# Second MLP: the order of matrix products and output tiles on TensorE, per pair of chunks

## The chip, the cores and the metric

The program runs on one core of one Trainium2 chip. The metric is the device time of one execution in microseconds (us), the median of the runs shown. The core has five engines that run side by side: TensorE (PE in the profile; its weight loads are listed apart as PEld), VectorE (DVE), ScalarE (ACT), GpSimd (POOL) and SyncE (SP), which issues the DMAs here. Each engine works through its own list of instructions in order, and semaphores hold an instruction back until what it needs is there.

## What is computed

Attention with a linear kernel, whose result is the input of a first MLP, whose result is the input of a second one. The change lies in the second MLP alone.

```python
def _moe2_ref(x, w_in, w_out):          # x 4608 x 512, w_in 512 x 2048, w_out 2048 x 512
    h = x @ w_in
    g = h * (1.0 / (1.0 + np.exp(-1.702 * h)))
    return (g @ w_out).astype(np.float32)
```

## The kernel before, in words

**Precision.** A float32 product is made of three matmuls of split operands: each operand is kept as a high part (`to_hi`, a copy on ACT) and a low part (`to_lo`, a subtraction on DVE or POOL), and `three` (L616) issues high by high, high by low, low by high. So every row `x3` or `x6` of TensorE is one or two products of 128x128 weights.

**Tokens and chunks.** The second MLP goes over 4608 tokens in six blocks of 768 (`NB2`), each of two halves of 384 tokens (`TH`). The 2048 columns of `w_in` are 16 chunks of 128, taken in eight pairs (`NQ`). A step of the work is one pair of chunks of one block; the text calls it pair n, n from 0 to 47, and pairs 8, 16, 24, 32 and 40 are the first of blocks 1 to 5.

**The first layer of a pair.** `x @ w_in` for 2 by 2 blocks (two halves of tokens, two chunks) is made with seven products instead of eight, on sums and differences of the operands. `steps_l1` (L764) lists them with their times in units of `PT` (2.2 us): the products a11, s2, a12, s3, s1, a22, s4, of six matmuls of 384 columns each. They accumulate in two PSUM buffers of the pool `ps_h` (two buffers, tag "h"), in three tiles per pair: bank 0 takes a11, then a12; bank 1 takes s2, s3 and a22; a second bank-0 tile takes s1 and s4. In the profile the first is called pa, the others ps. Between two products on one tile DVE or ACT reads the intermediate sum:

- `m1` (L798, ACT) copies a11's result; `add` (L805, DVE) makes c12 from bank 1 after s2, c22 from bank 1 after s3 and once more from bank 0 after s1, c21 from bank 1 after a22, c12 again from bank 0 after s4.
- `act` (L816, L817) is the activation of each of c11, c22, c21, c12: a sigmoid on ACT, a multiplication on DVE. `split` makes the high and low part of g, called gc in the profile (ACT and POOL, L134 and L137).

A product that goes on in a tile must wait until the read before it is done, and a product that begins a tile waits for the last reader of the buffer's tile before.

**The second layer.** While pair n's products run, the g blocks of pair n - 1 are multiplied by `w_out`: `unit` (L857) is one token tile (128 tokens) of one g block: three matmuls of 512 columns, added to one of six accumulators in PSUM (tiles 0 to 2 for the first half of the tokens, 3 to 5 for the second). A pair has twelve units, in the order c11 (tiles 0 to 2), c22 (3 to 5), c12 (0 to 2), c21 (3 to 5). The table `UNITS` (L1008) gives each of the twelve a time in `PT`, and so the place among the products.

**The end of a block.** In pairs 8, 16, 24, 32 and 40 the units finish the block before: tiles 0 to 2 with c12, tiles 3 to 5 with c21. `put_2` (L878), called right behind each unit's place, copies a finished tile to SBUF, even tiles on ACT (L892), odd ones on DVE (L894), and issues the DMA to the output.

**What sets the order.** Every step is put in a list with a time (`at`, L143); L1021 sorts the list by time and calls the steps in that order. So the times move instructions in all five lists of instructions, but no engine looks at them when it runs.

**Around the first pairs.** Other work shares the engines in pairs 0 to 8: the last sums and splits of the first layer's weights (`steps_q`, L295), the splitting of `w_out` (`steps_o`, L273: load, high on ACT, low on POOL, store), and in pairs 7, 15, 23 and so on the sums and splits of the next block's tokens (`steps_s`, L704).

Of the kernel before, what the change touches and what calls it, by code (L numbers as in the profile page):

```python
# [58 lines left out]
def kernel(  # L59
# [73 lines left out]
    def to_hi(hi, src):  # L133
        nc.scalar.activation(hi, src, AF.Copy)  # L134

    def to_lo(lo, src, hi, eng=nc.vector):
        eng.tensor_tensor(out=lo, in0=src, in1=hi.bitcast(F32), op=ALU.subtract)  # L137
# [5 lines left out]
    def at(t, fn, *args):  # L143
        plan.append((t, len(plan), fn, args))
# [471 lines left out]
    def three(out, w, x, start, stop, shared=False):  # L616

        for e, (a, b) in enumerate(((0, 0), (0, 1), (1, 0))):
            nc.tensor.matmul(  # L619
                out, w(a), x(b), start=(start and e == 0), stop=(stop and e == 2), skip_group_check=shared  # L620
            )
# [142 lines left out]
    def steps_l1(n):  # L764


        st = {}
        i, j = divmod(n, NQ)

        def product(bank, x, begin):  # L770
            def run():
                if begin:
                    st[bank] = ps_h.tile([P, TB], F32, tag="h", name=f"p{x}_{n}")
                a, at0 = W_AT[x]
                w, xs = wt[a, j], x_t["2", i, x]
                for k in range(2):
                    cs = slice(at0 + k * P, at0 + (k + 1) * P)
                    three(
                        st[bank][:, :TH],
                        lambda e: w[:, e, cs],  # L780
                        lambda e: xs[:, e, k, :],
                        begin and k == 0,
                        k == 1,
                        shared=True,
                    )

            return run

        def tile_(name):
            pool, tag = dict(  # L790
                m1=(late, "m1"), c12=(late, "c12"), c22=(late, "c22"), c21=(None, "t"), c11=(None, "t"), s=(None, "g")
            )[name]
            pool = cpool if pool is None else late["pool"]
            return pool.tile([P, TH], F32, tag=tag, name=f"{name}_{n}", bufs=2 if tag in ("c12", "t", "g") else 1)

        def m1():
            st["m1"] = tile_("m1")
            nc.scalar.activation(st["m1"], st[0][:, :TH], AF.Copy)  # L798

        def add(name, bank, to):  # L800
            def run():
                other = st[to]
                if name not in st:
                    st[name] = tile_(name)
                nc.vector.tensor_tensor(out=st[name], in0=st[bank][:, :TH], in1=other, op=ALU.add)  # L805

            return run

        def act(name):
            def run():  # L810
                if name == "c11":
                    h = st[0][:, :TH]
                    sig = st[name] = tile_(name)
                else:
                    h, sig = st[name], tile_("s")
                nc.scalar.activation(sig, h, AF.Sigmoid, scale=1.702)  # L816
                nc.vector.tensor_tensor(out=st[name], in0=h, in1=sig, op=ALU.mult)  # L817

            return run

        def split(name):
            def run():

                last = (name == "c12") == (n % 2 == 0) and name in ("c12", "c21")
                pool, tag = (late["pool"], "g4") if last else (gpool, "g")
                g = pool.tile([P, 2, TH], F32R, tag=tag, name=f"g{name}_{n}")
                to_hi(g[:, 0, :], st[name])
                to_lo(g[:, 1, :], st[name], g[:, 0, :], nc.gpsimd)
                g_t["2", n, name] = g

            return run

        return [
            (0.0, product(0, "a11", True)),
            (0.48, m1),
            (1.0, product(1, "s2", True)),
            (1.5, add("c12", 1, "m1")),
            (2.0, product(0, "a12", False)),
            (2.5, act("c11")),
            (3.0, product(1, "s3", False)),  # L840
            (3.1, split("c11")),
            (3.5, add("c22", 1, "m1")),
            (4.0, product(0, "s1", True)),
            (4.5, add("c22", 0, "c22")),
            (4.55, act("c22")),
            (5.0, product(1, "a22", False)),
            (5.1, split("c22")),
            (5.5, add("c21", 1, "m1")),
            (5.55, act("c21")),
            (6.0, product(0, "s4", False)),  # L850
            (6.1, split("c21")),
            (6.5, add("c12", 0, "c12")),
            (6.55, act("c12")),
            (7.1, split("c12")),
        ]
# [43 lines left out]
    with tc.manual_schedule():  # L899
# [11 lines left out]
        def when(t0, times, steps):  # L911
            for t, fn in zip(times, steps.values(), strict=True):
                at(t0 + t, fn)
# [82 lines left out]
        for i in range(NB2):  # L996
# [5 lines left out]
            else:  # L1002
# [2 lines left out]
                times += [0.6 * PT if i < 2 else quad(NQ * i - 2) + 3.7 * PT - t]  # L1005
                times += [e * PT for e in (0.5, 1.55, 2.55, 1.6, 3.6, 4.6, 5.6, 6.6)]
                when(t, times, steps_s(i))
        UNITS = [0, 0, 1, 1, 2, 2, 3, 3, 4, 4, 5, 6]  # L1008
        for n in range(NB2 * NQ + 1):
            if n < NB2 * NQ:  # L1010
                for dt, fn in steps_l1(n):
                    at(quad(n) + dt * PT, fn)
                for e in range(2 if n >= NQ else 0):
                    at(quad(n) + (0.3 + 0.1 * e) * PT, load_o, n // NQ, 2 * (n % NQ) + e)
            if n:
                order = ("c11", "c22", "c12", "c21") if n < NB2 * NQ else ("c11", "c22", "c21", "c12")
                todo = [(c, t) for c in order for t in range(NT2 // 2)]
                for e, (c, t) in zip(UNITS, todo, strict=True):
                    at(quad(n) + (e + 0.47) * PT, unit, n - 1, c, t)
                    at(quad(n) + (e + 0.49) * PT, put_2)  # L1020
# [32 lines left out]
```

## Time and profile before

| | |
|---|---|
| median of 3 runs | 1681.07 us (1680.23 to 1681.24) |
| the profiled execution, from its first to its last instruction (span) | 1678.0 us |
| TensorE busy in it | 1637.8 us, 98% |
| DVE, ACT, POOL busy | 935.7, 670.4, 697.7 us (56%, 40%, 42%) |
| second MLP: first product, last matmul's end | 907.2, 1674.1 us |

A row of the timeline reads: start in us from the span's start, duration in us, engine, line, operation, out<-in by the program's names with numbers left out, shape, how many equal instructions follow each other, and in square brackets the idle time of the engine before and what ended it. Matmuls overlap: the duration of a group runs to the end of its last one, so the pace is read from start to start. A row of the windows view reads: the stretch, its length, then TensorE's busy time and number of instructions (or all engines'), the granted TensorE clock as a share of full speed (PEclk), the DMA share and GB/s.

### The profile page before, as it was taken

How to read it: one execution, taken by the hardware profiler on the slowest of the kernel's cores; microseconds unless marked ns; L12 is line 12 of the kernel's file. 1: busy time of each engine (PE TensorE's matmuls, PEld its weight loads, DVE VectorE, ACT ScalarE, POOL GpSimd, SP SyncE). 2: the span in 40 equal slices, each digit the busy share in tenths (PEclk: the TensorE clock that was granted, in tenths of full speed). 3: DMA queues.
4: the chain of work that ended last, by engine and by line, in shares of the span. 5: the costliest groups of instructions: out<-in, count | busy, mean ns of one | idle time of the engine just before them, and what ended most of it. 6: DMA issues, size and time to landing. Idle time of an engine off the chain costs nothing.

```text
span 1678.0 us, 21576 instructions
## 1 busy us (share of the span) xinstructions
PE 1637.8 (98%) x7848; PEld 1407.0 (84%) x7848; DVE 935.7 (56%) x1647; ACT 670.4 (40%) x1228; POOL 697.7 (42%) x589
## 2 busy tenths in 40 slices
PE   6889999999999999999999999999999999999999
PEld 5667888888888888888887898888888888898897
DVE  8985767767676766666456434334334334334333
ACT  5655443444444444443434334324324324324322
POOL 4656333343334333333478546225225235235222
PEclk9989999999999999999999999999999999999999
DMA  7652323233322223211222323412412412412212
GB/s 214 186 155 75 96 65 106 74 100 90 105 81 80 85 83 96 66 57 50 75 78 82 143 88 113 151 51 77 150 51 80 146 51 82 144 52 84 104 53 86
DMA packets 127914, 159.75 MB, mean 95 GB/s; under 512 B 54080, under 2 KB 90944, under 8 KB 127808
## 3 DMA queue, kind: packets, MB, share of 16 engines
q1 hardware_dynamic: 127808, 158.37, 29.1%
q8 instruction: 62, 1.02, 0.2%
q14 instruction: 44, 0.36, 0.1%
HBM read 122.68 MB, written 35.65 MB: 94 GB/s over the span
## 4 chain that ended last, share of the span: by engine, by line
PE 84%; DVE 2%; POOL 2%; issue 2%; ACT 1%; DMA 1%; SPq 0%; POOLq 0%; ACTq 0%; DVEq 0%
PE acc L619 42%; PE ph L619 20%; PE ps L619 14%; PE pa L619 5%; PE px L574 1%; PE pk L440 1%; DVE qt L537 1%; POOL gc L137 1%; DMA to<-wod 0%; DVE c L817 0%; POOL wo L137 0%; ACT s L134 0%; DVE o L675 0%; DVE a L137 0%; ACT s L816 0%
## 5 line engine op out<-in xcount | busy, mean ns | idle before, releaser
L619 PE MATMUL acc<-wo,gc 128*128 128x512 f32 x1728 | 453.4, 394 | 0.0
L619 PE MATMUL acc<-g,wo 128*128 128x512 f32 x1728 | 423.2, 394 | 2.2 <-DVE to L209 0.9
L619 PE MATMUL ph<-x,wi 128*128 128x512 f32 x1728 | 422.5, 393 | 0.1
L619 PEld LDWEIGHTS acc<-g,wo 128*128 128x128 f32 x1728 | 324.2, 189 | 71.1 <-POOL g L137 1.5
L619 PEld LDWEIGHTS ph<-x,wi 128*128 128x128 f32 x1728 | 322.0, 189 | 67.3 <-PE warm L940 0.2
L137 POOL TENSOR_TENSOR gc<-c,gc 128x384 fp32r<-128x384 f32 x192 | 201.1, 1049 | 422.6 <-ACT gc L134 416.1
L619 PEld LDWEIGHTS acc<-wo,gc 128*128 128x128 f32 x1728 | 319.3, 188 | 46.1
L137 POOL TENSOR_TENSOR g<-g,g 128x512 fp32r<-128x512 f32 x144 | 195.9, 1360 | 382.2 <-ACT g L134 342.7
L134 ACT ACTIVATE g<-g 128x512 fp32r<-128x512 f32 x144 | 90.9, 631 | 207.0 <-DVE g L644 206.9
L805 DVE TENSOR_TENSOR c<-ps,m 128x384 f32<-128x384 f32 x144 | 80.2, 557 | 165.6 <-PE ps L619 152.8
L644 DVE TENSOR_TENSOR g<-g 128x512 f32<-128x512 f32 x128 | 108.3, 846 | 112.7 <-ACT g L638 110.3
L817 DVE TENSOR_TENSOR c<-c,s 128x384 f32<-128x384 f32 x144 | 100.4, 697 | 101.2 <-ACT s L816 101.2
L134 ACT ACTIVATE gc<-c 128x384 fp32r<-128x384 f32 x192 | 101.0, 526 | 135.9 <-DVE c L817 133.2
L816 ACT ACTIVATE s<-c 128x384 f32<-128x384 f32 x144 | 75.5, 524 | 193.9 <-DVE c L805 191.6
L638 ACT ACTIVATE g<-ph 128x512 f32<-128x512 f32 x144 | 85.6, 595 | 156.9 <-PE ph L619 154.2
L537 DVE STREAM_TRANSPOSE qt<-q 32x128 f32<-32x128 f32 x448 | 135.5, 302 | 5.7
L619 PE MATMUL pa<-a,w 128*128 128x384 f32 x576 | 117.2, 338 | 3.1 <-DVE c L805 1.8
L619 PE MATMUL ps<-s,wa 128*128 128x384 f32 x576 | 115.9, 335 | 2.4 <-DVE c L805 2.4
L619 PEld LDWEIGHTS pa<-a,w 128*128 128x128 f32 x576 | 103.0, 188 | 13.9 <-ACT m L798 3.0
L619 PEld LDWEIGHTS ps<-s,wa 128*128 128x128 f32 x576 | 102.9, 188 | 11.6 <-DVE c L805 3.2
L805 DVE TENSOR_TENSOR c<-ps,c 128x384 f32<-128x384 f32 x96 | 53.3, 555 | 67.1 <-PE ps L619 67.1
L817 DVE TENSOR_TENSOR c<-pa,c 128x384 f32<-128x384 f32 x48 | 26.7, 556 | 91.0 <-ACT c L816 90.4
(114 smaller groups left out, 1695.6 us busy)
## 6 DMA issues: line engine op xcount, KB each, us to landing
wo<-wod SPq DMA_DIRECT2D x80, 512.0 KB, 4.0
rawi<-in_moe_w_in_dram SPq DMA_DIRECT2D x32, 512.0 KB, 4.4
rawo<-in_moe_w_out_dram SPq DMA_DIRECT2D x32, 512.0 KB, 3.9
y<-o SPq DMA_DIRECT2D x36, 256.0 KB, 2.8
out_dram<-o SPq DMA_DIRECT2D x36, 256.0 KB, 2.0
k<-in_k_dram SPq DMA_DIRECT2D x32, 256.0 KB, 4.0
vt<-in_v_dram SPq DMA_DIRECT2D x64, 128.0 KB, 3.1
wod<-wo SPq DMA_DIRECT2D x16, 512.0 KB, 2.8
```

The lines of the kernel that those rows point to most:

```text
L134: nc.scalar.activation(hi, src, AF.Copy)
L137: eng.tensor_tensor(out=lo, in0=src, in1=hi.bitcast(F32), op=ALU.subtract)
L440: nc.tensor.matmul(st["pk"][:, :VW], st["ke"][:, j, :], st["v"][:, j, :], start=(j == 0), stop=(j == KJ),)
L537: nc.vector.transpose(out=st["qt"][32 * g : 32 * g + 32, a * P : (a + 1) * P].rearrange("d (j t) -> d j t", j=QJ), in_=st["qn"][32 * a : 3 ...
L574: nc.tensor.matmul(st["px"][:, cols], a, c[:, cols], start=(e == 0), stop=(e == 2))
L619: nc.tensor.matmul(out, w(a), x(b), start=(start and e == 0), stop=(stop and e == 2), skip_group_check=shared)
L638: nc.scalar.activation(st["g"], st["h"], AF.Relu)
L644: nc.vector.tensor_tensor(out=st["g"], in0=st["g"], in1=st["g"], op=ALU.mult)
L805: nc.vector.tensor_tensor(out=st[name], in0=st[bank][:, :TH], in1=other, op=ALU.add)
L816: nc.scalar.activation(sig, h, AF.Sigmoid, scale=1.702)
L817: nc.vector.tensor_tensor(out=st[name], in0=h, in1=sig, op=ALU.mult)
```

## The change

The times of three products in `steps_l1` move so that each stands right behind the product before it, and `UNITS` puts the three token tiles of one g block together. The order becomes: a11, s2, three units of c11; a12, s3, three of c22; s1, a22, three of c12; s4, three of c21. Nothing is added or removed.

```diff
@@ steps_l1
             (0.0, product(0, "a11", True)),
             (0.48, m1),
-            (1.0, product(1, "s2", True)),
+            (0.4, product(1, "s2", True)),
             (1.5, add("c12", 1, "m1")),
             (2.0, product(0, "a12", False)),
             (2.5, act("c11")),
-            (3.0, product(1, "s3", False)),
+            (2.4, product(1, "s3", False)),
             (3.1, split("c11")),
             (3.5, add("c22", 1, "m1")),
             (4.0, product(0, "s1", True)),
             (4.5, add("c22", 0, "c22")),
             (4.55, act("c22")),
-            (5.0, product(1, "a22", False)),
+            (4.4, product(1, "a22", False)),
...
-        UNITS = [0, 0, 1, 1, 2, 2, 3, 3, 4, 4, 5, 6]
+        UNITS = [0, 0, 0, 2, 2, 2, 4, 4, 4, 6, 6, 6]
```

On TensorE, the first ten groups of pair 16. The names: pa11, ps2 and ps1 are the three tiles of the first layer; after the arrow stands the product's operand (a11, s2, ...); acc2 with block and token tile is an accumulator, gc11 and so on the g block with its pair. Before:

```order
L619 MATMUL pa11_16_10068<-a11_2_9949,w10_7394 128x384 x6
L619 MATMUL acc2_1_0_9213<-wo2_1_14_9937,gc11_15_9995 128x512 x3
L619 MATMUL acc2_1_1_9217<-wo2_1_14_9937,gc11_15_9995 128x512 x3
L619 MATMUL ps2_16_10090<-s2_2_9967,wq0_7488 128x384 x6
L619 MATMUL acc2_1_2_9230<-wo2_1_14_9937,gc11_15_9995 128x512 x3
L619 MATMUL acc2_1_3_9234<-wo2_1_15_9939,gc22_15_10035 128x512 x3
L619 MATMUL pa11_16_10068<-a12_2_9986,w10_7394 128x384 x6
L619 MATMUL acc2_1_4_9246<-wo2_1_15_9939,gc22_15_10035 128x512 x3
L619 MATMUL acc2_1_5_9250<-wo2_1_15_9939,gc22_15_10035 128x512 x3
L619 MATMUL ps2_16_10090<-s3_2_10006,wa0_7449 128x384 x6
```

TensorE, the same place now:

```order
L619 MATMUL pa11_16_10068<-a11_2_9959,w10_7394 128x384 x6
L619 MATMUL ps2_16_10080<-s2_2_9964,wq0_7488 128x384 x6
L619 MATMUL acc2_1_0_9220<-wo2_1_14_9937,gc11_15_9995 128x512 x3
L619 MATMUL acc2_1_1_9224<-wo2_1_14_9937,gc11_15_9995 128x512 x3
L619 MATMUL acc2_1_2_9228<-wo2_1_14_9937,gc11_15_9995 128x512 x3
L619 MATMUL pa11_16_10068<-a12_2_9992,w10_7394 128x384 x6
L619 MATMUL ps2_16_10080<-s3_2_10000,wa0_7449 128x384 x6
L619 MATMUL acc2_1_3_9248<-wo2_1_15_9946,gc22_15_10032 128x512 x3
L619 MATMUL acc2_1_4_9252<-wo2_1_15_9946,gc22_15_10032 128x512 x3
L619 MATMUL acc2_1_5_9256<-wo2_1_15_9946,gc22_15_10032 128x512 x3
```

s2 and s3 have moved ahead of two units each; the units now stand in threes.

On DVE, the end of a block, in pair 16 (the same rows stand in pairs 8, 24, 32 and 40; o2 is an output tile's copy). Before:

```order
L805 TENSOR_TENSOR c12_16_10103<-ps2_16_10090,m1_16_10088 128x384
L817 TENSOR_TENSOR c11_16_10117<-pa11_16_10068,c11_16_10117 128x384
L894 COPY o2_1_1_10138<-acc2_1_1_9217 128x512
L805 TENSOR_TENSOR c22_16_10141<-ps2_16_10090,m1_16_10088 128x384
L894 COPY o2_1_10156<-acc2_1_3_9234 128x512
L805 TENSOR_TENSOR c22_16_10141<-ps1_16_10143,c22_16_10141 128x384
L817 TENSOR_TENSOR c22_16_10141<-c22_16_10141,s_16_10162 128x384
L805 TENSOR_TENSOR c21_16_10180<-ps2_16_10090,m1_16_10088 128x384
L817 TENSOR_TENSOR c21_16_10180<-c21_16_10180,s_16_10182 128x384
L894 COPY o2_1_5_10197<-acc2_1_5_9250 128x512
L805 TENSOR_TENSOR c12_16_10103<-ps1_16_10143,c12_16_10103 128x384
```

DVE, the same place now:

```order
L805 TENSOR_TENSOR c12_16_10100<-ps2_16_10080,m1_16_10098 128x384
L817 TENSOR_TENSOR c11_16_10123<-pa11_16_10068,c11_16_10123 128x384
L805 TENSOR_TENSOR c22_16_10129<-ps2_16_10080,m1_16_10098 128x384
L894 COPY o2_1_1_10156<-acc2_1_1_9224 128x512
L805 TENSOR_TENSOR c22_16_10129<-ps1_16_10131,c22_16_10129 128x384
L817 TENSOR_TENSOR c22_16_10129<-c22_16_10129,s_16_10163 128x384
L805 TENSOR_TENSOR c21_16_10169<-ps2_16_10080,m1_16_10098 128x384
L817 TENSOR_TENSOR c21_16_10169<-c21_16_10169,s_16_10171 128x384
L894 COPY o2_1_10159<-acc2_1_3_9248 128x512
L894 COPY o2_1_5_10197<-acc2_1_5_9256 128x512
L805 TENSOR_TENSOR c12_16_10100<-ps1_16_10131,c12_16_10100 128x384
```

The copy of tile 1 has moved from ahead of c22's first addition to ahead of its second, and the copy of tile 3 from ahead of that second addition to ahead of the copy of tile 5. ACT's list changes in one place per block end: its copy of tile 4 has moved behind c21's sigmoid and high part. Outside the five block ends the lists of DVE and ACT are the same, and those of POOL and SP are the same throughout.

## Rows read from the trace of the kernel before

**Rows 1.** The page: the span, and the engines' busy time (TensorE's line).

```profile
span 1678.0 us, 21576 instructions
...
PE 1637.8 (98%) x7848; PEld 1407.0 (84%) x7848; DVE 935.7 (56%) x1647; ACT 670.4 (40%) x1228; POOL 697.7 (42%) x589
```

**Rows 2.** Windows, all engines, 100 us within the second MLP.

```profile
1100.00:1200.00 100.00, 100.00 (x498) 89.78 (x497) 41.32 (x65) 35.77 (x69) 40.14 (x33) 1.00 0.29 106
```

**Rows 3.** Timeline, pair 16 from its first product to the next pair's, TensorE.

```profile
1163.77 1.22 PE L619 MATMUL pa<-a,w 128*128 128x384 f32 x6
...
1164.83 1.55 PE L619 MATMUL acc<-wo,gc 128*128 128x512 f32 x6
...
1166.22 1.21 PE L619 MATMUL ps<-s,wq 128*128 128x384 f32 x6
...
1167.26 1.55 PE L619 MATMUL acc<-wo,gc 128*128 128x512 f32 x6
...
1178.76 0.86 PE L619 MATMUL acc<-wo,gc 128*128 128x512 f32 x3
...
1179.45 1.22 PE L619 MATMUL pa<-a,w 128*128 128x384 f32 x6
```

**Rows 4.** Timeline, TensorE: longer runs of matmuls of 512 columns (pair 0; the end).

```profile
916.12 2.92 PE L619 MATMUL acc<-g,wo 128*128 128x512 f32 x12
...
1669.66 4.47 PE L619 MATMUL acc<-wo,gc 128*128 128x512 f32 x19
```

**Rows 5.** Timeline, the end of a block in pair 16: units, DVE's copy, additions.

```profile
1172.13 1.55 PE L619 MATMUL acc<-wo,gc 128*128 128x512 f32 x6
...
1173.72 0.69 DVE L894 COPY o<-acc 128x512 f32<-128x512 f32 x1 [2.68 <-PE acc L619]
1174.32 0.55 DVE L805 TENSOR_TENSOR c<-ps,m 128x384 f32<-128x384 f32 x1
...
1176.76 0.55 DVE L805 TENSOR_TENSOR c<-ps,c 128x384 f32<-128x384 f32 x1
...
1177.96 0.56 DVE L817 TENSOR_TENSOR c<-c,s 128x384 f32<-128x384 f32 x1 [0.65 <-ACT s L816]
1178.44 0.55 DVE L805 TENSOR_TENSOR c<-ps,m 128x384 f32<-128x384 f32 x1
```

**Rows 6.** Timeline, pair 8: s2 of TensorE waits for DVE's addition.

```profile
1039.40 0.55 DVE L805 TENSOR_TENSOR c<-ps,c 128x384 f32<-128x384 f32 x1
...
1040.00 1.31 PE L619 MATMUL ps<-s,wq 128*128 128x384 f32 x6 [0.47 <-DVE c L805]
...
1041.16 1.55 PE L619 MATMUL acc<-wo,gc 128*128 128x512 f32 x6
```

**Rows 7.** Timeline, pairs 1 to 4: DVE, ACT, and each pair's start on TensorE.

```profile
932.37 0.54 DVE L805 TENSOR_TENSOR c<-ps,m 128x384 f32<-128x384 f32 x1
...
941.44 1.22 PE L619 MATMUL pa<-a,w 128*128 128x384 f32 x6
...
955.10 0.63 ACT L134 ACTIVATE wo<-to 128x512 fp32r<-128x512 f32 x1 [5.56 <-DMA to<-wod]
...
958.04 1.31 PE L619 MATMUL pa<-a,w 128*128 128x384 f32 x6 [0.76 <-DVE c L805]
...
959.59 0.55 DVE L805 TENSOR_TENSOR c<-ps,c 128x384 f32<-128x384 f32 x1
...
974.18 1.22 PE L619 MATMUL pa<-a,w 128*128 128x384 f32 x6
```

**Rows 8.** Timeline, pair 7: its start on TensorE, and DVE's first addition.

```profile
1021.24 1.22 PE L619 MATMUL pa<-a,w 128*128 128x384 f32 x6
...
1027.11 0.55 DVE L805 TENSOR_TENSOR c<-ps,m 128x384 f32<-128x384 f32 x1
```

**Rows 9.** Windows, TensorE alone: a stretch of pair 1, and one early in the program.

```profile
925.00:935.00 10.00, 8.17 (x39) 1.00 0.13 52
100.00:120.00 20.00, 16.03 (x60) 0.83 0.47 126
```

## Prediction

> **What bounds the kernel now.** I read the page first: TensorE is busy for 1637.8 of 1678.0 us [rows 1]. Then the windows: in the second MLP a stretch of 100 us shows TensorE busy for 100.00 at a granted clock of 1.00, with the other engines at 36 to 41 [rows 2]. So between pair 9 and the end the program runs at TensorE's pace; a new order of its work can gain there only by a better pace from matmul to matmul, and can lose wherever a wait appears. Third, the timeline, for that pace. A pair takes 1179.45 - 1163.77 = 15.68 us: a product is 1.04 to 1.07 (1166.22 to 1167.26, for one), six matmuls of two units 1.39 (1164.83 to 1166.22), one unit 0.69 [rows 3]. Seven products at 1.05 and five double units at 1.39 and two single ones at 0.69 make 15.68, the whole pair: no idle time is left in it.
>
> **The change, part by part.** The same 78 matmuls per pair stay; only their neighbours change.
>
> *Pace.* A run of matmuls of 512 columns gets faster as it goes on. With about 0.39 us for the last one's own duration (x3 is 0.86 = 0.39 + 2 x 0.235), x6 gives (1.55 - 0.39)/5 = 0.232 each [rows 3], x12 (2.92 - 0.39)/11 = 0.230 and x19 (4.47 - 0.39)/18 = 0.227 [rows 4]. Three units in a row, nine matmuls, lie between 1.39 + 0.69 = 2.08 and 1.39 + 3 x 0.227 = 2.07. Four such runs take about 8.30 where 5 x 1.39 + 2 x 0.69 = 8.33 stood: 0.03 to 0.04 per pair, and over some 41 undisturbed pairs **-1.4 us** (bounds 0 and -3).
> The Trainium skill, "TensorE: Matmul & The Clock Gate", section "Back-to-back issue gap", gives the gap of a matmul from its columns alone (N/2.4 + 2.5 ns, which is 216 ns at 512), without regard to its neighbours. The trace does not agree with the figure (227 to 235 ns), nor with the independence; by that rule this term would be 0 and the sum 1688.7.
>
> *Waits in an undisturbed pair.* I lay the new order out from a11 at T = 0 with 1.05 per product and 2.08 per three units: a11 0, s2 1.05, c11's units 2.10, a12 4.18, s3 5.23, c22's units 6.28, s1 8.36, a22 9.41, c12's units 10.46, s4 12.54, c21's units 13.59, next a11 15.67. Each product on a tile now has at least three units and a product (3.1 us) between it and the one before it, where two double units and a product (3.8) stood. What must fit in is one read: it starts 0.20 after the last matmul's pace slot, and TensorE goes on 0.60 after an addition's start (1039.40 to 1040.00 [rows 6]), 0.8 together; with ACT's m1 or a sigmoid ahead of it some 2. So nothing waits, and the cost is 0. That cover has a margin of about 1 us, and it is gone where DVE does something else first.
>
> *The end of a block, five times.* There DVE must also copy output tiles, in its list's order. Now the copy of tile 1 stands ahead of c22's second addition, which s4 waits for. The second of c12's units ends at T = 10.46 + 1.39 = 11.85; the copy starts 0.20 later (1172.13 + 1.39 = 1173.52, copy at 1173.72), the next addition 0.60 after it (1174.32) [rows 5]: 12.65, and TensorE's s4 at 13.25 where it is due at 12.54: 0.71. After such a wait the first product takes 1.16 (1040.00 to 1041.16 [rows 6]) in place of 1.05, so 0.82. What is late next: c22's multiplication 1.20 after the addition (1176.76 to 1177.96), c21's addition 0.48 on (1178.44) [rows 5], c21's multiplication again 1.20 on: 15.53. Behind it now stand two copies, of tiles 3 and 5; the last unit ends at 13.25 + 1.16 + 2.08 = 16.49, so the copy of tile 5 starts at 16.69, c12's second addition at 17.29, and the next pair's s2, which takes that buffer, at 17.89 where it is due at 16.49 + 1.05 = 17.54: 0.35, with the restart 0.46. ACT's copies and a11's buffer (free at 14.9) don't come later than these. 5 x 1.28 = **+6.4 us** (bounds: 5 x 0.71 = 3.5 with one wait and no restart; 5 x 1.88 = 9.4 if one more copy, 0.60, lies in the way).
>
> *Pairs 1 to 3.* In pair 1 DVE makes the last weights' sums ahead of c12's first addition at 932.37 [rows 7], whatever TensorE does, so s3 begins at 932.97 in both orders. Before, six units were done by then, and 8.47 us were left to the pair's end at 941.44; now s3 stands right behind a12, only three are done, and three more units, 2.08, come after it: pair 2 begins at 943.5. In pair 2 ACT waits for a DMA until 955.10, and that chain held back pair 3's a11 to 958.04 (0.76 idle) [rows 7]; now a11 is due at 943.5 + 15.67 = 959.2, after it, so most of the loss is swallowed. But s2 stands right behind a11 now, due at 960.2, and its buffer is read by the addition of 959.59 [rows 7], which I put some 0.3 later since s4 of pair 1 is 0.7 later: s2 at 960.5, 0.3 and a restart of 0.11. From there 15.67 - 1.05 to pair 4, 975.2 against 974.18 [rows 7]: **+1.0 us** (bounds 0 and 2.1, the three units).
>
> *Pairs 7 and 8.* The next block's sums share DVE. c12's first addition of pair 7 starts 1027.11 - 1021.24 = 5.87 after the pair [rows 8]; s3 was due later than that (three products and three double units, 7.3), now at 5.23. The chain ahead of it can be earlier by up to two units, 1.39, since s4 of pair 6 is; so s3 loses between 0 and 1.3, and pair 8's s2, which waited already [rows 6] and is due two units sooner, about as much, while the later wait of that pair goes. I take **+0.2** in all (bounds -1 and +2).
>
> *Sum.* -1.4 + 6.4 + 1.0 + 0.2 = +6.2 on the profiled span of 1678.0, 1684.2; the median of the runs is 3.1 above that span (1681.07), so **1687.3 us**, slower by 0.37%. About 0.2%, 3.4 us, is what a measurement can tell from no change.
>
> **The rivals.**
> *The pace wins (faster).* If the longer runs bring both kinds of matmul to their settled pace at once, units cost 36 x 0.227 and products 42 x 0.173 (1.04/6): 15.44 per pair, -0.24, over 47 pairs -11.3; with the waits, 1681.07 + 7.6 - 11.3 = 1677.4. It decides from -0.19 per pair (7.6 over 41). For it: the x19 row. Against: x12 still pays 0.230 on the mean, and nine is shorter. Chance 0.06.
> *The copies hold nothing (no change to be told).* If the copy of tile 1 is done before s4 needs its sum, the five block ends cost nothing: 1681.07 + 1.2 - 1.4 = 1680.9. Against: DVE's list is in order, and its copies wait for TensorE [rows 5]. Chance 0.15.
> *Waits in each pair.* If DVE and POOL get in each other's way and every pair loses 0.1, 41 x 0.1 more: 1691.4. Against: the margin of 1 us. Chance 0.07.
> *The clock falls in pair 1.* s3's wait grows there to about 2.6 us. Early in the program, in a stretch with idle time, the granted clock is 0.83 over 20 us; in pair 1 it stays 1.00 with 1.83 idle in 10 [rows 9]. A mean of 0.83 between full and half clock is 6.8 us at half, worth 3.4: 1690.7. The Trainium skill, "TensorE: Matmul & The Clock Gate", section "What's actually happening", says that TensorE's clock is throttled by default and that activity releases it; the first of the two rows agrees, the second shows that idle time of this kind need not suffice. Chance 0.06.
> *No gain in pace.* If nine matmuls in a row cost what six and three cost apart, 2.08, the first term is 0, its upper bound: 1688.7. Against: the means of x6, x12 and x19 [rows 3, 4]. This is where the Trainium skill's rule on the gap ("TensorE: Matmul & The Clock Gate", section "Back-to-back issue gap") would lead. Chance 0.06.
> The forecast keeps 0.60.
>
> **How the numbers follow.** Likeliest 1687.3; its own bounds, not all at one end, 1683 to 1690. The range takes in the case without held copies (down to 1680.5) and most of the slower cases (up to 1691.0); it leaves out the faster rival and the tails. Faster by over 0.2%: the first rival and a little, 0.07. Within 0.2%: the second rival, and the forecast with its low bounds, 0.18. Slower: 0.75.
>
> **What would show it.** In the profile after: undisturbed pairs 15.64 to 15.67 from a11 to a11; units of a group in 2.07 to 2.08; in pairs 8, 16, 24, 32 and 40 TensorE idle before s4 and before the next pair's s2, both ended by DVE's additions (L805), behind copies (L894); pair 2's a11 about 2 us later than before, pair 4's about 1. The prediction is wrong if the windows show TensorE busy throughout at the block ends, if pairs take over 15.75, or if they fall below 15.5.

## The result, and the profile after

The changed kernel takes **1691.92 us** (median of five runs, 1691.28 to 1692.96) against 1681.07: ratio 1.0065, 95% interval 1.0053 to 1.0078, slower by 0.65%. The forecast was slower too, 1687.3, and its range ended at 1691.0, 0.9 below the result. The profiled execution spans 1689.5 us, 11.5 more than before; the medians differ by 10.9.

The page, its span and the busy times, answering to [rows 1]:

```profile
span 1689.5 us, 21541 instructions
...
PE 1641.8 (97%) x7848; PEld 1409.8 (83%) x7848; DVE 947.6 (56%) x1647; ACT 674.0 (40%) x1228; POOL 700.3 (41%) x589
```

TensorE is busy for 4.0 us more with the same instructions, and idle for the other 7.5. The view of waits, TensorE, 900 to 1690 us, says for whom (us in total, times, longest; its largest row):

```profile
PE ps L619 <- DVE c L805: 10.5, 15, 1.5
```

In the kernel before, the same view has 2.9 us and three waits in this row. So products on the ps tiles now wait for DVE's additions 15 times, ten of them at the five block ends. Windows, TensorE alone, show that there is no wait between the block ends (compare [rows 2]):

```profile
1060.00:1160.00 100.00, 100.00 (x498) 1.00 0.26 94
```

The timeline, TensorE, pair 18, one of the undisturbed ones (compare [rows 3]):

```profile
1201.22 1.23 PE L619 MATMUL pa<-a,w 128*128 128x384 f32 x6
1202.29 1.20 PE L619 MATMUL ps<-s,wq 128*128 128x384 f32 x6
1203.33 2.24 PE L619 MATMUL acc<-wo,gc 128*128 128x512 f32 x9
1205.41 1.23 PE L619 MATMUL pa<-a,w 128*128 128x384 f32 x6
...
1216.93 1.23 PE L619 MATMUL pa<-a,w 128*128 128x384 f32 x6
```

From start to start: a11 takes 1.07, s2 1.04, three units 2.08, the pair 15.71, where it took 15.68 to 15.69.

The end of a block in pair 16, all engines, the rows of [rows 5] in their new order:

```profile
1178.66 2.25 PE L619 MATMUL acc<-wo,gc 128*128 128x512 f32 x9
...
1180.25 0.69 DVE L894 COPY o<-acc 128x512 f32<-128x512 f32 x1 [4.95 <-PE acc L619]
1180.86 0.55 DVE L805 TENSOR_TENSOR c<-ps,c 128x384 f32<-128x384 f32 x1
...
1181.46 1.32 PE L619 MATMUL ps<-s,wbb 128*128 128x384 f32 x6 [0.55 <-DVE c L805]
...
1182.54 0.55 DVE L805 TENSOR_TENSOR c<-ps,m 128x384 f32<-128x384 f32 x1
...
1183.32 1.01 POOL L137 TENSOR_TENSOR gc<-c,gc 128x384 fp32r<-128x384 f32 x1 [6.88 <-ACT gc L134]
1183.74 1.01 DVE L817 TENSOR_TENSOR c<-c,s 128x384 f32<-128x384 f32 x1 [0.65 <-ACT s L816]
...
1184.67 1.27 DVE L894 COPY o<-acc 128x512 f32<-128x512 f32 x2
1184.70 1.22 PE L619 MATMUL pa<-a,w 128*128 128x384 f32 x6
...
1185.86 0.54 DVE L805 TENSOR_TENSOR c<-ps,c 128x384 f32<-128x384 f32 x1
...
1186.46 1.32 PE L619 MATMUL ps<-s,wq 128*128 128x384 f32 x6 [0.54 <-DVE c L805]
```

c12's units begin at 1178.66, so s4 is due 2.08 later, 1180.74; it starts at 1181.46, 0.72 late, behind the copy of tile 1 and the addition. s2 is due 1.06 behind a11, 1185.76; it starts at 1186.46, 0.70 late, behind two copies and c12's addition. Each restart adds 0.11.

Where the 11.5 us lie, from the starts of a11 in both timelines:

| stretch | after - before | forecast |
|---|---|---|
| up to pair 1 (923.28, now 924.53) | +1.25 | 0 |
| pairs 1 to 3 (to pair 4: 974.18, now 976.16) | +0.73 | +1.0 |
| pairs 4 to 6 | +0.06 | in the pace |
| pairs 7 and 8, without the block end | +0.36 | +0.2 |
| block end of pair 8: 0.83 + 1.06 | +1.89 | +1.28 |
| four later block ends, 1.63 each | +6.5 | +5.1 |
| the other 30 pairs, 0.02 each | +0.7 | -1.4 |

The first line is not the change's, since the order of the program is the same up to there: the second MLP began at 907.2 us before, at 908.6 after, and between 906.2 and 908.8 in the profiles of the eleven kernels below, which have the same program ahead of it too. The rest is 10.2, where the forecast had 6.2.

### The profile page after: what moved, and what is told of

Its sections match the earlier page's. It is cut to its first block, busy times and chain, and to the rows that moved or that the text cites. A ratio compares the mean times of both kernels' runs of the same rounds, so it can differ in the third digit from the quotient of the medians.

```text
span 1689.5 us, 21541 instructions
## 1 busy us (share of the span) xinstructions
PE 1641.8 (97%) x7848; PEld 1409.8 (83%) x7848; DVE 947.6 (56%) x1647; ACT 674.0 (40%) x1228; POOL 700.3 (41%) x589
## 3 DMA queue, kind: packets, MB, share of 16 engines
q8 instruction: 62, 1.02, 0.2%
## 5 line engine op out<-in xcount | busy, mean ns | idle before, releaser
L619 PE MATMUL acc<-wo,gc 128*128 128x512 f32 x1728 | 430.4, 393 | 0.0
L817 DVE TENSOR_TENSOR c<-c,s 128x384 f32<-128x384 f32 x144 | 113.1, 786 | 98.8 <-ACT s L816 98.8
L805 DVE TENSOR_TENSOR c<-ps,m 128x384 f32<-128x384 f32 x144 | 79.8, 554 | 92.5 <-PE ps L619 80.8
L805 DVE TENSOR_TENSOR c<-ps,c 128x384 f32<-128x384 f32 x96 | 53.3, 555 | 103.5 <-PE ps L619 103.5
L817 DVE TENSOR_TENSOR c<-pa,c 128x384 f32<-128x384 f32 x48 | 26.7, 556 | 119.8 <-ACT c L816 119.1
```

Source lines behind the costliest of these rows:

```text
L619: nc.tensor.matmul(out, w(a), x(b), start=(start and e == 0), stop=(stop and e == 2), skip_group_check=shared)
```

## The experiments

They ran in three groups, each beside the kernel before on the same chip (1680.89, 1680.39 and 1680.27 us there). The ratios below are to that kernel. The **theory**: waits at the block ends come from the order of DVE's list, and every group of units costs TensorE something for the change of shape. The **rivals**: the grouping itself costs the time; or the waits are only handed from place to place.

**1. All copies behind the additions.** The changed kernel with

```diff
-                    at(quad(n) + (e + 0.49) * PT, put_2)
+                    at(quad(n) + (e + 0.51) * PT, put_2)
```

> The changed kernel, with the output copies of a finished block placed just behind the additions that TensorE waits for (c22's second and c12's second) instead of just ahead of them. Theory A (the copies stand in DVE's list ahead of those additions and cost 1.6 us at each of five block ends): 1691.9 - 5 x 1.63 = about 1683.7, no TensorE wait on DVE at the block ends. Rival B (the pace from matmul to matmul, or work before the second MLP, makes most of the loss): within 1 us of 1691.9.

Measured: 1686.29 us, ratio 1.0029 (1.0017 to 1.0040). The waits at s4 are gone, and each later block end costs 0.35 in place of 1.63 (pairs of 16.05 us). What is left is s2 of the next pair, 0.24 late with a restart: no copy stands ahead of c12's addition any more, but c21's multiplication does, and it takes 1.00 (see run 8). DVE and TensorE in pair 17:

```profile
1184.64 1.00 DVE L817 TENSOR_TENSOR c<-c,s 128x384 f32<-128x384 f32 x1 [0.65 <-ACT s L816]
...
1186.16 1.31 PE L619 MATMUL ps<-s,wq 128*128 128x384 f32 x6
```

Pair 1 took 21.77 us, in which the changed kernel takes 20.22, although the lists of all engines are the same there. Timeline, TensorE, and windows of the same stretch:

```profile
934.81 1.69 PE L619 MATMUL ps<-s,wa 128*128 128x384 f32 x6 [2.46 <-DVE c L805]
936.30 3.48 PE L619 MATMUL acc<-wo,gc 128*128 128x512 f32 x9
```

```profile
935.00:937.00 2.00, 2.00 (x8) 0.64 0.00 0
937.00:939.00 2.00, 2.00 (x6) 0.51 0.48 98
```

Three units take 3.32 (936.30 to s1 at 939.62) in place of 2.08: after 2.46 us without work the granted clock was near its lower level, 0.5. The profiled execution took 1687.15 us, 3.4 above the expectation: some 1.5 of that are clock in pair 1, and 1.9 are the waits that are left, 0.35 at each of four block ends and 0.7 at pair 8's.

**2. The grouping alone.** The kernel before with the new `UNITS`, its products where they were. TensorE's order is then a11, three units, s2 a12, three, s3 s1, three, a22 s4, three.

> The kernel before with the new table of units alone: three units of one g block stand together, and the pairs of neighbouring products are s2 and a12, s3 and s1, a22 and s4. Theory A (it is the product moved ahead, not the grouping, that exposes the reads): a12 stands between s2 and s3, a22 between s1 and s4, so block ends and pairs 1 to 3 lose nothing, and only the pace remains, 0.02 to 0.03 us per pair: 1681 to 1683. Rival B (the grouping of units costs by itself): 1688 or more.

Measured: 1680.42 us, ratio 0.9998 (0.9989 to 1.0007). A steady pair takes 15.71, as after the change, and from pair 9 on nothing waits. Yet DVE, ACT and POOL go through the same instructions in the same order here as in the changed kernel, with the copies ahead of the additions. Only TensorE's order differs: s4 has a22 ahead of it (1.05 us), the next pair's s2 three units (2.08), and that is more than the waits of 0.72 and 0.70. So neither the groups of three, nor two products side by side, nor the copies' new places make the loss by themselves; it takes the copies ahead of the additions together with products that stand too close behind them.

**3. Groups of four.** The changed kernel, with

```diff
-        UNITS = [0, 0, 0, 2, 2, 2, 4, 4, 4, 6, 6, 6]
+        UNITS = [0, 0, 0, 0, 2, 2, 2, 2, 4, 4, 4, 4]
...
-                    at(quad(n) + (e + 0.49) * PT, put_2)
+                    at(quad(n) + {0: 0.51, 2: 3.51, 4: 6.51}[e] * PT, put_2)
```

> The new order of products, with the twelve units in three runs of four, and the output copies placed behind the additions. It measures the pace of longer runs: fewer switches between products and units. Theory A (each switch costs a settling time; a run of nine matmuls and the product behind it cost 0.067 us over the settled pace): with three switches of some 0.05 to 0.07 a pair takes 15.58 to 15.65 us, and the whole 1680 to 1684. Rival B (a settling cost that grows with the run): pairs of 15.71 or more, 1685 or more.

Measured: 1686.31 us, ratio 1.0035 (1.0023 to 1.0048). A steady pair takes 15.64: three groups are better than four by 0.07. Pairs 1 to 3 took 53.94 us (51.63 after the change), with half clock in 935 to 938 again, and s2 of the pairs 16, 24, 32 and 40 still waits (0.69), here for an addition behind a split of the next block's tokens on DVE. So the pace came as expected, and the time, 2.3 above the expected range, did not.

**4. The old order up to pair 8**, the changed one from pair 9:

```diff
+        OLD_UNITS = [0, 0, 1, 1, 2, 2, 3, 3, 4, 4, 5, 6]
...
+                for e, (c, t) in zip(OLD_UNITS if n <= 8 else NEW_UNITS, todo, strict=True):
```

(the three products' times likewise).

> The changed kernel with the old order (products and units) in pairs 0 to 8, the new one from pair 9 on. Theory A (pairs 1 to 9 cost 3.0 us of the whole: 0.7 in pairs 1 to 3, 0.8 in pair 7, 1.5 in pairs 8 and 9): 1688.9. Rival B (what starts before the second MLP makes the difference, 1.3 us in the two profiles, and the early pairs nothing more): 1691.9.

Measured: 1689.28 us, ratio 1.0050 (1.0038 to 1.0063). Pairs 10 to 46 take 587.6 us, as after the change (587.64; 580.45 before). So 7.2 of the loss arise there, from the block ends and the pace; the pairs before give the rest. The old order there saves 2.5 of them (8.4 above the kernel before in place of 10.9), though pair 9, the first in the new order, now takes 17.08 where it took 16.78.

**5. Groups of four from pair 9**, the copies and that split behind the additions, the old order up to pair 8.

> Old order in pairs 0 to 8. From pair 9 the changed products with the units in three groups of four (a11 s2 4 a12 s3 4 s1 a22 4 s4), each copy of an output tile behind the addition that TensorE waits for, and the split of the next block's last block of tokens behind c12's last addition. Theory (a group of matmuls pays about 0.02 to 0.03 us for every change of shape, and waits at block ends come only from the order of DVE's list): a steady pair takes 15.64, 0.05 less than before, over 39 pairs -2 us, no wait of TensorE on L805 is left from pair 9 on, and the time is 1679 us. Rival (the new order of products costs TensorE a wait at block ends whatever DVE's list): the pairs 16, 24, 32 and 40 keep 0.35 or more each, and the time is 1680.5 or more.

Measured: 1680.24 us, ratio 0.9998 (0.9990 to 1.0007). From pair 10 every pair takes 15.64 to 15.65, block ends too; the rival is out. What was missed is pair 9: its s2 waits 1.07, behind the last copies of block 0, which still stood in their old place: 1.3 of the 2 us that were expected.

**6. Groups of six from pair 9**: a11 s2 a12 s3, six units, s1 a22 s4, six units.

> Old order in pairs 0 to 8. From pair 9 only two groups of units per pair: a11 s2 a12 s3, six units, s1 a22 s4, six units, with the copies behind the additions. Theory (every change of shape costs, so that two in a pair are cheaper than four; the reads between the products fit into 1.05 us each, the duration of the product in between): a pair takes 15.55 to 15.60, over 39 pairs -4 to -5 us, the time is 1676 to 1677 us. Rival (the reads of a tile between two products, about 0.8 us from the last matmul with DVE free, meet DVE busy with other work in most pairs): TensorE waits 0.1 us or more in each pair, the windows show it idle, and the time is 1681 or more.

Measured: 1689.06 us, ratio 1.0048 (1.0034 to 1.0061). A middle pair takes 15.60, as the theory has it, with no wait. But s4 of the pairs 15, 23, 31 and 39 waits for an addition behind the next block's splits (16.61 to 16.63 us), and a12 of the pairs 17, 25, 33 and 41 for ACT's m1, which stands behind a copy and a high part (16.81 to 16.85): eight times 1.0 to 1.3, and pair 9 takes 18.1. The rival is right in these pairs alone.

**7. Only the copies of tiles 3 to 5 behind the addition.** The changed kernel, with

```diff
-                    at(quad(n) + (e + 0.49) * PT, put_2)
+                    at(quad(n) + (6.51 if e == 6 else e + 0.49) * PT, put_2)
```

> The changed kernel with one place altered: the copies of tiles 3 to 5 at a block's end stand behind c12's second addition (time 6.51 in place of 6.49). Theory (each of the two waits of a block end has its own copy ahead of it): the wait at s4 stays at 0.7 and its restart, the wait at the next pair's s2 falls from 0.7 to about 0, and the five block ends give back 5 x 0.8 = 4.0: 1687.9 us. Rival (s2 is late because s4's wait delays the whole chain of additions and multiplications, and the copies only lie beside it): s2 still waits 0.3 or more, and the time is 1690 us or more.

Measured: 1686.43 us, ratio 1.0035 (1.0022 to 1.0048). The same block end, DVE and TensorE:

```profile
1182.12 1.00 DVE L817 TENSOR_TENSOR c<-c,s 128x384 f32<-128x384 f32 x1 [0.66 <-ACT s L816]
1183.05 0.54 DVE L805 TENSOR_TENSOR c<-ps,c 128x384 f32<-128x384 f32 x1
1183.52 1.27 DVE L894 COPY o<-acc 128x512 f32<-128x512 f32 x2
```

```profile
1179.84 1.32 PE L619 MATMUL ps<-s,wbb 128*128 128x384 f32 x6 [0.55 <-DVE c L805]
...
1183.09 1.23 PE L619 MATMUL pa<-a,w 128*128 128x384 f32 x6
1184.16 1.20 PE L619 MATMUL ps<-s,wq 128*128 128x384 f32 x6
```

s4 waits as before; s2 follows a11 after 1.07, no wait. Pair 17 takes 15.71 in place of 16.52. So each wait has its own copies ahead of it. c21's multiplication is as slow here, and does no harm because s4's wait has put off the next a11 by 0.8; in run 1, where s4 is on time, it alone makes s2 0.24 late.

**8. c22's split a step later.** The changed kernel, with

```diff
-            (5.1, split("c22")),
+            (5.56, split("c22")),
```

> The changed kernel with c22's split (high part on ACT, low part on POOL) a step later, behind c21's sigmoid, so that POOL's subtraction for c22 no longer runs beside DVE's multiplication for c21. Theory (that multiplication takes 1.01 us at the block ends and not 0.56 because POOL's subtraction runs at the same time, and the 0.45 us are what made the wait at s2 0.70 where I had forecast 0.35): the multiplication takes 0.56 there, s2 waits about 0.35, and the time is 1691.9 - 5 x 0.35 = 1690.2 us. Rival (the multiplication is slow for another reason, or is not on the way to s2): s2 still waits 0.7 and the time is 1691.9 us.

Measured: 1687.40 us, ratio 1.0042 (1.0029 to 1.0054). The same block end: POOL, then DVE, then TensorE.

```profile
1181.71 1.98 POOL L137 TENSOR_TENSOR gc<-c,gc 128x384 fp32r<-128x384 f32 x2 [7.76 <-PE acc L619]
```

```profile
1181.25 0.56 DVE L817 TENSOR_TENSOR c<-c,s 128x384 f32<-128x384 f32 x1 [0.65 <-ACT s L816]
1181.73 1.38 DVE L894 COPY o<-acc 128x512 f32<-128x512 f32 x2
1183.02 0.55 DVE L805 TENSOR_TENSOR c<-ps,c 128x384 f32<-128x384 f32 x1
```

```profile
1182.21 1.22 PE L619 MATMUL pa<-a,w 128*128 128x384 f32 x6
1183.62 1.32 PE L619 MATMUL ps<-s,wq 128*128 128x384 f32 x6 [0.19 <-DVE c L805]
```

POOL's subtraction now begins 0.46 behind the multiplication's start, and the multiplication takes 0.56. s2 is due at 1183.27 and starts at 1183.62: 0.35 late, the forecast's own number. The block ends give 2.0 us (pair 8's 0.6, the others' 0.36 each); another 1.3 comes from pair 1 (18.88 us in place of 20.22), which the expectation had not seen: ACT reaches the sigmoids of pair 0's c21 and c12 sooner there (by 0.5 and 1.6, counted from pair 1's a11), and DVE's sums of the last weights, and s3 behind them, come 1.36 sooner after a11.

**9. Groups of four from pair 10**, otherwise as 5; `OLD_UNITS` and the old times hold for `n <= 9`:

```diff
+        OLD_UNITS = [0, 0, 1, 1, 2, 2, 3, 3, 4, 4, 5, 6]
+        NEW_UNITS = [0, 0, 0, 0, 2, 2, 2, 2, 4, 4, 4, 4]
+        PUTS = {0: 0.51, 2: 3.51, 4: 6.51}
```

> As the run with the old order to pair 8 and groups of four from pair 9, but with the old order to pair 9 and groups of four from pair 10. There pair 9's s2, put right behind a11, waited 1.07 us for the addition that stands behind block 0's last copies. Theory (that wait came only from the change of order at a block end): pair 9 takes 15.69 as before, pairs 10 to 47 take 15.64 and wait nowhere, 37 x 0.05 = 1.9 us less than before: 1678.5 us. Rival (the place of the change does not matter, the first pair in the new order always waits): pair 10 takes about 17.0 and the time is 1679.8 us.

Measured: **1678.25 us**, ratio 0.9990 (0.9981 to 0.9999): faster than both kernels, by 2.0 us of 1680.27. Of this the pairs 10 to 46 give 1.65 (578.80 us in place of 580.45). Pair 9 takes 15.68, no later pair over 15.67. A group of four in the timeline of TensorE, where the product behind twelve matmuls takes 1.07 again:

```profile
1201.97 2.92 PE L619 MATMUL acc<-wo,gc 128*128 128x512 f32 x12
1204.73 1.23 PE L619 MATMUL ps<-s,wa 128*128 128x384 f32 x6
1205.80 1.20 PE L619 MATMUL ps<-a,wq 128*128 128x384 f32 x6
```

**10. Groups of six in the middle pairs, of four elsewhere.**

> Old order to pair 9; from pair 10 groups of six units (a11 s2 a12 s3, six units, s1 a22 s4, six units) in the five middle pairs of each block, groups of four in the pairs 15, 16, 17, 23, 24, 25 and so on, where the next block's sums and the output's copies share DVE and ACT and where groups of six lost 1.0 to 1.3 us. Theory (each group of nine or more units' matmuls costs about 0.07 us over the settled pace, and nothing waits in the middle pairs): 25 pairs at 15.60, 12 at 15.64, 2.8 us less than before: 1677.6 us. Rival (the change between the two orders costs a wait each time): eight changes of 0.3 us or more bring it back to 1680 or above.

Measured: 1682.24 us, ratio 1.0010 (1.0001 to 1.0019). The middle pairs take 15.60, but the first of each run of middle pairs (10, 18, 26 and so on) 16.4 to 16.6: a12, which now stands two products behind a11, waits for ACT's m1, and ACT's list has the last g block of the pair before ahead of it. That block's high part is itself late, behind a multiplication on DVE that takes 1.01 beside POOL's subtraction (1069.56). The rival is right, with five changes that cost 0.8 to 1.0.

```profile
1070.67 0.53 ACT L134 ACTIVATE gc<-c 128x384 fp32r<-128x384 f32 x1 [1.14 <-DVE c L817]
...
1071.10 0.47 ACT L798 ACTIVATE m<-pa 128x384 f32<-128x384 f32 x1
...
1071.62 1.33 PE L619 MATMUL pa<-a,w 128*128 128x384 f32 x6 [0.51 <-ACT m L798]
```

**11. Both repairs at once**: the changed kernel with the edits of 1 and 8, TensorE's groups as the change has them.

> The changed kernel with two repairs at once and its order of TensorE's groups untouched: the copies of output tiles stand behind the additions that TensorE waits for, and c22's split stands behind c21's sigmoid. Theory (the change lost 8.4 us to the two waits at each of five block ends and less than 3 us to everything else): both waits are gone at pairs 16, 24, 32 and 40, whose pairs take 15.7, pair 1 ends 1.3 us earlier too, as it did with the split alone, and the time is 1682 us, 1 to 2 above the kernel before, since a pair takes 15.71 in place of 15.69. Rival (the two orders of DVE's list only hand the wait from one place to another): a wait of 0.3 us or more at each block end is left, and the time is 1684 us or more.

Measured: 1681.61 us, ratio 1.0009 (1.0001 to 1.0018). Every pair from 9 on takes 15.71. In pair 16 the additions (c22's second, then c12's) now stand ahead of the copies, and neither s4 nor s2 waits; first DVE, then TensorE:

```profile
1172.82 0.56 DVE L805 TENSOR_TENSOR c<-ps,c 128x384 f32<-128x384 f32 x1 [2.52 <-PE ps L619]
1175.25 0.69 DVE L894 COPY o<-acc 128x512 f32<-128x512 f32 x1 [1.87 <-PE acc L619]
...
1179.14 0.55 DVE L805 TENSOR_TENSOR c<-ps,c 128x384 f32<-128x384 f32 x1
1179.61 1.28 DVE L894 COPY o<-acc 128x512 f32<-128x512 f32 x2
```

```profile
1175.74 1.23 PE L619 MATMUL ps<-s,wbb 128*128 128x384 f32 x6
...
1178.89 1.23 PE L619 MATMUL pa<-a,w 128*128 128x384 f32 x6
1179.96 1.20 PE L619 MATMUL ps<-s,wq 128*128 128x384 f32 x6
```

So two edits of DVE's, ACT's and POOL's lists take back 9.5 of the 10.9 us (1.3 above the kernel before, ratio 1.0009 in place of 1.0065) and leave TensorE's order as the change made it. About 1.3 of the 9.5 are pair 1's, as in run 8; the block ends give the larger part.

## Why the prediction was wrong, point by point

**Right: the sign, the places, and the first wait.** TensorE waits before s4 and before the next pair's s2 at all five block ends, each time for L805 behind copies of L894. The first was forecast at 0.71 and is 0.72. Run 1 takes away the first and run 7 the second, each by moving the copies ahead of it; run 2 shows that the copies cost nothing where TensorE's products stand further behind.

**Mis-sized: the second wait, +2.0 us.** The step that failed reads "c21's multiplication again 1.20 on: 15.53. Behind it now stand two copies ... 0.35". The start was right: addition at 1182.54, multiplication at 1183.74. But I priced both multiplications by c22's row of 0.56 [rows 5], and c21's takes 1.01 here, since POOL subtracts for c22 from 1183.32 on. So the two copies start only 0.93 behind it, at 1184.67, and c12's addition at 1185.86, which is 17.68 after the pair's a11 where I had 17.29 (tile 5's copy behind its last unit); the wait is 0.70, not 0.35, in four block ends, and 0.95 in pair 8's, where a copy on ACT also holds c22's sigmoid back by 0.27. Run 8 shows it: with the multiplication at 0.56 the wait is 0.35. Even c21's own row at this block end, from the timeline of the kernel before, would not have told it, since POOL's subtraction (1179.21, 1.02 long) is nearly over there:

```profile
1180.07 0.58 DVE L817 TENSOR_TENSOR c<-c,s 128x384 f32<-128x384 f32 x1 [1.08 <-ACT s L816]
```

The profile had the sign of it: L817's mean over the whole kernel, in the view of lines, is 697 ns before and 786 after, well over 0.56 us. Over the whole trace after, 56 of these 144 multiplications start with POOL idle and take 0.56; the other 88 start while POOL is busy and take 0.56 to 1.42, 1.03 in the median. Before, the counts are 91 and 53, so the change also brought more of them beside POOL. An addition of L805, which reads PSUM and one operand in SBUF, is not touched: the one at 1044.54 takes 0.56 while POOL subtracts from 1043.06 on for 2.16. The Trainium skill, "SBUF — State Buffer", section "Who interferes with whom", says that a VectorE instruction with two SBUF inputs contends with a GpSimd instruction that reads SBUF, and that one with at most one SBUF input, outside its 2-port modes, does not. The trace agrees: the multiplication ends 0.42 behind the end of POOL's subtraction (1183.74 + 1.01 against 1183.32 + 1.01), and the addition takes 0.56.

**Wrong in sign: the pace, +0.7 in place of -1.4.** The step was "Seven products at 1.05" kept constant while only the units changed. The units did what I wrote (2.08 for nine matmuls). From the starts between 1200 and 1290 us, the medians of a stretch of TensorE's work in us:

| | before | after | four (run 3) | six (run 6) |
|---|---|---|---|---|
| units | 5 x 1.389 + 2 x 0.698 | 4 x 2.081 | 3 x 2.761 | 2 x 4.121 |
| products | 5 x 1.044 + 2 x 1.062 | 3 x 2.106 + 1.066 | 2 x 2.106 + 3.146 | 3.146 + 4.212 |
| pair | 15.69 | 15.71 | 15.64 | 15.60 |

A product takes 1.044 behind six matmuls of units, but 1.062 to 1.066 behind three, nine or more; the second of two neighbours takes 1.04. Four of a pair's seven products now stand behind nine. That is +0.04 per pair, which the units' -0.02 does not cover. Why six is the exception, no run here shows, nor why the fourth of four neighbours in run 6 takes 1.064 again. From nine on each further group costs 0.04 to 0.07, so fewer are faster: 15.60, 15.64, 15.71 for two, three, four. The Trainium skill, "TensorE: Matmul & The Clock Gate", section "Back-to-back issue gap", gives the gap of an isolated matmul by a formula of its columns alone. The trace does not agree for a stream of them, since the same product of 384 columns takes 1.044 or 1.066 by what stands ahead of it. By that formula this term is 0, which is nearer to what was measured than mine.

**Near: the early pairs.** Pair 2's a11 comes 2.05 later than before, counted from pair 1's (forecast 2.08), and pair 4's 0.73 (forecast 1.0). The timeline of pair 1, TensorE and DVE, for [rows 7]:

```profile
926.72 2.29 PE L619 MATMUL ps<-s,wq 128*128 128x384 f32 x6 [0.86 <-DVE c L805]
...
933.58 0.54 DVE L805 TENSOR_TENSOR c<-ps,m 128x384 f32<-128x384 f32 x1
...
934.18 1.31 PE L619 MATMUL ps<-s,wa 128*128 128x384 f32 x6 [1.52 <-DVE c L805]
...
944.75 1.23 PE L619 MATMUL pa<-a,w 128*128 128x384 f32 x6
```

s3 waits for the addition behind the weights' sums, as I had it. The wait of 0.3 that I put at pair 3's s2 did not come: s2 follows a11 there after 1.07, which is why pair 4 loses 0.73 and not 1.0. In pairs 7 and 8, s3 of pair 7 is now 0.67 late, 0.8 with its restart, which lay in the bounds, and the later wait of pair 8 (0.35 and its restart) goes.

```profile
1029.20 1.31 PE L619 MATMUL ps<-s,wa 128*128 128x384 f32 x6 [0.52 <-DVE c L805]
```

**The rivals.** The copies hold back TensorE, so that case is out, and so are the waits in each pair: the window between block ends is full, and every pair there takes 15.71. "No gain in pace" is what that term came to, and a little worse; it had 0.06. The clock did fall in pair 1, with no cost there: windows, TensorE alone,

```profile
927.00:929.00 2.00, 2.00 (x7) 0.50 0.43 176
929.00:931.00 2.00, 2.00 (x9) 0.75 0.21 86
```

show half clock in s2 and the first of c11's units, and s3 waits for DVE until 934.18 in any case. Pair 1 takes 20.22 us here and 20.22 in run 7, whose clock stayed at 1.00. In run 1 the fall came later, behind s3's wait, and cost some 1.5, where that rival had 3.4. The forecast was 4.6 too low: 2.0 are the second wait and 2.1 the pace, and the misses in the early pairs (-0.3 and +0.2) cancel. The last 0.6 are not the change's: the second MLP began later (+1.25 at pair 1), and the median lies 2.4 above the profiled span and not 3.1 (-0.7). Both mis-sized terms point the same way; I had not let the pace and the copies miss together.

## What to carry to other kernels

Where an engine's list is in order, look at what stands ahead of each instruction that the bounding engine waits for. Here one copy that nobody waits for held TensorE up by 0.7 us, and by nothing when it stood one place later (run 1) or when one more product stood ahead of the waiting one (run 2). Price an operation with what the neighbour engines will do beside it in the new order, not by an undisturbed row: the same multiplication took 0.58 at its block end before the change and 1.01 after. When groups on TensorE are made longer, count what the first instruction behind a group pays as well as what the group saves.

## What the runs showed of the hardware that was not expected

- DVE's multiplication of 128x384 (operands in SBUF) takes 0.56 us alone and 1.01 where POOL subtracts at the same time; in run 8, where POOL starts 0.46 later than the multiplication, it takes 0.56. DVE's additions of the same shape, with one operand in PSUM, take 0.54 to 0.56 either way. With both repairs the multiplication's mean over the kernel, from the view of lines, falls to 618 ns:

```profile
L817 DVE TENSOR_TENSOR c<-c,s 128x384 f32<-128x384 f32 x144 | 88.9, 618 | 95.2 <-ACT s L816 95.2
```

- The granted clock at the start of the second MLP differs between executions of nearly the same work: TensorE fell to 0.5 behind waits of 1.12 and 0.86 us in the changed kernel and behind 2.46 us in run 1, and stayed at 1.00 behind 1.10, 0.86 and then 2.47 us in run 7. What decides it is open.
- A product of six matmuls of 384 columns pays 0.02 us for standing behind three, nine, twelve or eighteen matmuls of 512 columns, and not behind six.
